# Retention of blocks 3 to 5 in 64x64 tiles: chunks worked by halves, in two groups of products

## The chip, the cores and the metric

One Trainium2 chip, one of its cores. The metric is the device time of one execution in microseconds. A core has five engines that run side by side, each in its own order: TensorE (PE: matmuls, and their weight loads, PEld), VectorE (DVE), ScalarE (ACT), GpSimd (POOL) and SyncE (SP), which here issues nearly all DMAs. Matmuls read SBUF and write PSUM.

## What is computed

Three layers in a row on 4 x 768 tokens of 512 values. The first is retention, 8 heads of 64 values each, one state per batch and head:

```python
for t in range(S):
    state = gamma * state + einsum('bhd,bhe->bhde', k[:, :, t], v[:, :, t])
    y[:, :, t] = scale * einsum('bhd,bhde->bhe', q[:, :, t], state)
```

Its output x (3072 x 512) goes through `g(x @ w_in) @ w_out` twice, w_in 512 x 2048 and w_out 2048 x 512. In layer 0 of the two g is a quotient of polynomials, `P(h) / (Q(h) + 1e-6)`; in layer 1 it is `h * clip(h + 3, 0, 6) / 6`.

## The kernel before

**Steps.** Tokens are worked in six blocks of 512 (NBLK), the 2048 inner columns in 16 tiles of 128 (FT). A step is one (layer, block, tile): `emit_h` (L359) makes h, 128x512 in PSUM, with 12 matmuls of 512 columns, and two steps later (LAG) `emit_o` (L371) adds the product of g with w_out into four accumulators with 12 more. Twelve and not four, since every operand is split into a rounded high part and a rest (xh, xl; gh, gl; two halves of each weight) and three of the four products are made. The steps stand in one list: 96 of layer 0, then 96 of layer 1. In layer 0 DVE and ACT turn h into g: ACT L440 to L442, DVE L448, L449, L452, ACT L457, L458 (`s1_h`, `s1_pq`, `s1_r`, one step behind h), DVE L463 to L465, ACT L470 (gh), DVE L476 (gl) (`s1_g`, `s_hi`, `s_lo`, two steps behind). h has two PSUM buffers, gh and gl two each.

**Retention.** A block has four chunks of 128 tokens, a sequence six chunks, so among the 12 chunks of blocks 3 to 5 two are the first and two the last of a sequence. A chunk is loaded by five DMAs of 256 KB on SP (`att_load`, L183: q and k transposed, k, v and a table of decays). `att_q` (L213) and `att_v` (L218) scale q and v by the decays on DVE. `att_scores` (L230) makes k.q for the eight heads, tiles of 64 rows and 128 columns, into the two PSUM banks of tag "at"; `att_mask` (L241) takes the triangle of it to SBUF, 1024 columns on DVE. `att_out` (L259) makes mask x v (L272, tiles of 128 rows and 64 columns), the chunk's sum of k x v (L285, same tiles, not in the last chunk) and state x q (L300, tiles of 64x64, not in the first). `att_xh` (L325, ACT) and `att_xl` (L337, DVE) write the chunk's part of the block's xh and xl, and `att_state` (L344) adds the sum to the state in SBUF. These products are fp32, and each is two matmul instructions in the profile.

**Order.** The order is written out by hand. `chunk_at` (L589) files each part of a chunk under a step n and a place in the step's program; the loop from L706 emits, for step n: `emit_h(n)`; what is filed under `begin`; `s1_g`, `s_hi` of tile n-2; `middle`; `s1_pq` of n-1 with `s_lo` of n-2 in it; `s1_r`; `before`; `emit_o(n-2)`; `after`. A chunk of blocks 3 to 5 that is filed at step s has its loads at s-2, q and v at s-1 (`before`), scores behind `emit_o` of s, mask in `before` of s+1, outputs behind `emit_o` of s+1, xh in `begin` and xl and state in `before` of s+2. The next chunk comes four steps later. The chunks of block b are worked during the steps of the block ahead of it in the list: from step n0 = 32, 48 and 64 for blocks 3, 4 and 5. The x tiles have two slots, b % 2 for these blocks.

Of the kernel before, what the change touches and what calls it, by code (L numbers as in the profile page):

```python
# [7 lines left out]
F32 = mybir.dt.float32  # L8
# [3 lines left out]
AF = mybir.ActivationFunctionType  # L12
# [19 lines left out]
def tile_retention_moe_moe2(  # L32
# [179 lines left out]

    def att_q(blk, c):  # L213
        qT, kT, kr, vr, tq, ka = loaded.pop((blk, c))
        nc.vector.tensor_tensor(out=qT, in0=qT, in1=tq, op=ALU.mult)
        attn[blk, c] = (by_pair(qT), by_pair(kT), heads(kr), heads(vr), ka)

    def att_v(blk, c):  # L218
        vr = attn[blk, c][3]
        powers = tab_v[(blk * CPB + c) % CPS]  # L220
        if (1, 0) < (blk, c) < (VIA + 1, 0):

            for h in range(H):
# [35 lines left out]
    def att_out(blk, c):  # L259
        qT, kr, vr, am = attn.pop((blk, c))  # L260
        ci = (blk * CPB + c) % CPS
        first, last = ci == 0, ci == CPS - 1
        both, py = two_banks(blk, (2 * c + 1) % 3, f"py{blk}_{c}")

        def to(e, j, i):
            return py[e][i * 64 : (i + 1) * 64, j * CH : (j + 1) * CH]

        for j in range(2):
            for e in range(2):
                for i in range(2):  # L270
                    p = 2 * j + i
                    nc.tensor.matmul(  # L272
                        to(e, j, i),
                        lhsT=vr[:, 2 * p + e, :],
                        rhs=am[:, e * NP + p, :],
                        start=j == 0,
                        stop=first and j == 1,
                        skip_group_check=True,
                    )
        new = py[0][:, 256:512]  # L280

        def to_state():
            for p in range(NP):
                for e in range(2):
                    nc.tensor.matmul(  # L285
                        new[e * 64 : (e + 1) * 64, p * D : (p + 1) * D],
                        lhsT=kr[:, 2 * p + e, :],
                        rhs=vr[:, 2 * p + e, :],
                        start=False,
                        stop=True,  # L290
                        skip_group_check=True,
                    )

        def from_state():
# [13 lines left out]


        parts = ([] if last else [to_state]) + ([] if first else [from_state])  # L310
        for part in reversed(parts) if (blk, c) == (0, CPB - 1) else parts:
            part()
        attn[blk, c] = (both, new, first, last)

    XSLOT = {0: 1, 1: 0, 6: 0, 7: 1, 8: 1, 9: 0, 10: 1, 11: 0} | {b: b % 2 for b in range(2, 6)}

# [94 lines left out]
    def emit_evac(layer, blk, f):  # L411
        earlier = partial.pop((layer, blk), None)
        for j, ps in enumerate(acc.pop((layer, blk))):
            scale = G_SCALE if layer == 0 else 1.0 / 6.0
            if earlier:
                o = earlier[j]
                nc.vector.scalar_tensor_tensor(out=o, in0=ps, scalar=scale, in1=o, op0=ALU.mult, op1=ALU.add)
            else:
                o = out_tile(layer, blk, j, f"o{layer}_{blk}_{f}_{j}")
                if layer == 0 or j % 2 == 0:  # L420
                    nc.scalar.activation(o, ps, AF.Copy, scale=scale)
                else:
                    nc.vector.tensor_scalar(out=o, in0=ps, scalar1=scale, scalar2=None, op0=ALU.mult)
            t0 = blk * NB + j * 128
            if layer == 0:
                to = x2_dram[blk][j]
            else:
                to = out[t0 : t0 + 128, :] if f == FT - 1 else part_dram[j]
            nc.sync.dma_start(out=to, in_=o)

    def s1_h(key):
# [4 lines left out]
        p = t2.tile([128, NB], F32, tag="p", name=f"p{nm}")  # L439
        nc.scalar.activation(p, h, AF.Identity, scale=ab[:, 3:4], bias=ab[:, 2:3])  # L440
        nc.scalar.activation(s, h, AF.Square)
        nc.scalar.activation(u, h, AF.Abs, scale=ab[:, 4:5])  # L442
        tm[key] = [s, u, p]

    def s1_pq(key, between=None):
        s, u, p = tm[key]
        h = hps.pop(key)
        nc.vector.tensor_tensor(out=p, in0=p, in1=h, op=ALU.mult)  # L448
        nc.vector.scalar_tensor_tensor(out=u, in0=s, scalar=babs[:, 1:2], in1=u, op0=ALU.mult, op1=ALU.add)  # L449
        if between:  # L450
            between()
        nc.vector.scalar_tensor_tensor(out=p, in0=p, scalar=ab[:, 1:2], in1=h, op0=ALU.add, op1=ALU.mult)  # L452

    def s1_r(key):
        s, u, p = tm[key]
        r = t1.tile([128, NB], F32, tag="r", name=f"r{key[1]}_{key[2]}")
        nc.scalar.activation(r, u, AF.Ln, scale=1.0 / LN_SCALE, bias=ln_bias)  # L457
        nc.scalar.activation(r, r, AF.Exp, scale=-1.0)  # L458
        tm[key] = [u, p, r]

    def s1_g(key):
        u, p, r = tm[key]
        nc.vector.scalar_tensor_tensor(out=u, in0=u, scalar=Q_CONST, in1=r, op0=ALU.add, op1=ALU.mult)  # L463
        nc.vector.scalar_tensor_tensor(out=p, in0=p, scalar=ab[:, 0:1], in1=r, op0=ALU.add, op1=ALU.mult)  # L464
        nc.vector.scalar_tensor_tensor(out=p, in0=u, scalar=-2.0 * LN_SCALE, in1=p, op0=ALU.add, op1=ALU.mult)  # L465
        tm[key] = p

    def s_hi(key):
# [4 lines left out]
    def s_lo(key):  # L473
        gh = gsp[key]
        gl = g_p.tile([128, NB], F32R, tag="gl", name="gl" + "_".join(map(str, key)))
        nc.vector.tensor_tensor(out=gl, in0=tm.pop(key), in1=gh.bitcast(F32), op=ALU.subtract)  # L476
        gsp[key] = (gh, gl)


# [101 lines left out]
            made["lo"] += 1  # L581


    begin, middle, before, after, begun = {}, {}, {}, {}, []

    def put(where, n, fn, *args):
        where.setdefault(n, []).append((fn, *args))
# [1 line left out]
    def chunk_at(blk, c, s, loads=None):  # L589
# [9 lines left out]
        put(middle if blk <= VIA else begin, s + 2, att_xh, blk, c)  # L599
        put(before, s + 2, att_evac, blk, c)  # L600

    for c in range(CPB):
        chunk_at(1, c, 2 * c - 1, max(2 * c - 3, -1))
        chunk_at(VIA, c, CUT1 + 4 * c, CUT1 - 2 + 4 * c)
        for b in range(VIA + 1, NBLK):
            n0 = at_of[0, b - 1, 0] if b > VIA + 1 else 2 * FT
            chunk_at(b, c, n0 + 4 * c, n0 + 4 * c - 2)
# [88 lines left out]
    w_hi(*jobs[1])  # L696
    nc.scalar.activation(babs, ab[:, 4:6], AF.Abs)
    att_state(0, 3)
    for parts in (begin, middle, before, after):
        for n in sorted(n for n in parts if n < 0):  # L700
            for fn, *args in parts.pop(n):
                if fn is not att_load:
                    begun.append((fn, *args))

    late = []
    for n in range(len(steps) + LAG):  # L706
# [7 lines left out]
        if n == 0:  # L714
# [1 line left out]
            w_second()  # L716
            w_first()
            emit_h(at_step(1))
        if k1:
            (s1_h, s2_h)[k1[0]](k1)  # L720
# [5 lines left out]
        if k2 and k2[0] == 0:  # L726
            s1_g(k2)
            s_hi(k2)
        elif k2:
            s_lo(k2)  # L730
        for fn, *args in middle.get(n, ()):
            fn(*args)
        for key in late:
# [2 lines left out]
        late.clear()  # L736
        while made["lo"] < made["bits"]:
            w_second()
        rest = (lambda: s_lo(k2)) if k2 and k2[0] == 0 else None
        if k1 and k1[0] == 1:  # L740
            if rest:
                rest()
            s2_g(k1)
            s_hi(k1)
        if todo > 0:
            w_first()
        if k1 and k1[0] == 0:
# [93 lines left out]
```

## Time and profile before

| | before |
|---|---|
| median of 3 runs | 1170.14 us (1169.34 to 1170.98) |
| span of the profiled execution | 1169.4 us |
| PE busy, matmul instructions | 1142.6 us, 6028 |
| DVE busy, instructions | 754.3 us, 1174 |
| ACT busy, instructions | 640.2 us, 1091 |
| POOL busy | 32.6 us |

The profile is of one execution, from its first to its last instruction; its time is 0.7 us under the median of the runs. Busy time of PE counts a matmul from its start until its last result, and one starts while the one before is still draining; so starts, not durations, tell its pace. The timeline merges equal instructions that follow each other: a start, the time until the last of them ends, and their count.

### The profile page before, as it was taken

How to read it: one execution, taken by the hardware profiler on the slowest of the kernel's cores; microseconds unless marked ns; L12 is line 12 of the kernel's file. 1: busy time of each engine (PE TensorE's matmuls, PEld its weight loads, DVE VectorE, ACT ScalarE, POOL GpSimd, SP SyncE). 2: the span in 40 equal slices, each digit the busy share in tenths (PEclk: the TensorE clock that was granted, in tenths of full speed). 3: DMA queues.
4: the chain of work that ended last, by engine and by line, in shares of the span. 5: the costliest groups of instructions: out<-in, count | busy, mean ns of one | idle time of the engine just before them, and what ended most of it. 6: DMA issues, size and time to landing. Idle time of an engine off the chain costs nothing.

```text
span 1169.4 us, 15740 instructions
## 1 busy us (share of the span) xinstructions
PE 1142.6 (98%) x6028; PEld 931.0 (80%) x6028; DVE 754.3 (64%) x1174; ACT 640.2 (55%) x1091; POOL 32.6 (3%) x43
## 2 busy tenths in 40 slices
PE   8698999999999999999999999999999999999998
PEld 5566788888888888888888788888888888888886
DVE  6898898998888878888899865432332332332322
ACT  3898888866666566666888644332222332332222
POOL 0121110000000000000000000000000000000000
PEclk9898999999999999999999999999999999999999
DMA  9898643312112113121332643120200200200000
GB/s 334 246 263 211 183 114 95 135 53 74 46 46 82 46 55 117 46 81 37 108 99 64 227 136 106 36 90 1 72 1 1 72 1 1 72 1 1 36 1 36
DMA packets 59547, 100.20 MB, mean 86 GB/s; under 512 B 5328, under 2 KB 23888, under 8 KB 59472
## 3 DMA queue, kind: packets, MB, share of 16 engines
q1 hardware_dynamic: 54144, 89.50, 23.2%
q0 software_dynamic: 5328, 9.70, 4.8%
q8 instruction: 47, 0.77, 0.3%
q14 instruction: 28, 0.23, 0.1%
HBM read 73.76 MB, written 15.73 MB: 77 GB/s over the span
## 4 chain that ended last, share of the span: by engine, by line
PE 80%; ACT 8%; DVE 7%; DMA 2%; issue 2%; SPq 0%; ACTq 0%; DVEq 0%
PE h L368 38%; PE accA L392 19%; PE accB L392 19%; DMA T<-in_qk_t_dram 2%; PE sc L236 1%; PE py L272 1%; DVE u L463 1%; ACT r L457 1%; DVE p L464 1%; DVE p L448 1%; ACT r L458 1%; DVE u L449 1%; PE py L300 1%; ACT p L440 1%; ACT u L442 1%
## 5 line engine op out<-in xcount | busy, mean ns | idle before, releaser
L368 PE MATMUL h<-xh,wi 128*128 128x512 f32 x1536 | 416.4, 393 | 0.9 <-ACT xh L335 0.9
L368 PEld LDWEIGHTS h<-xh,wi 128*128 128x128 f32 x1536 | 285.8, 188 | 63.9 <-issue 2.7
L368 PE MATMUL h<-xl,wi 128*128 128x512 f32 x768 | 205.7, 390 | 0.0
L488 DVE SCALAR_TENSOR_TENSOR g<-r,h 128x512 f32<-128x512 f32 x96 | 66.1, 688 | 169.4 <-ACT r L482 168.7
L368 PEld LDWEIGHTS h<-xl,wi 128*128 128x128 f32 x768 | 144.3, 188 | 30.7
L482 ACT ACTIVATE r<-h,cst 128x512 f32<-128x512 f32 x96 | 66.0, 687 | 183.6 <-PE h L368 183.1
L470 ACT ACTIVATE gh<-g 128x512 fp32r<-128x512 f32 x96 | 60.7, 632 | 153.1 <-PE accB L392 113.9
L476 DVE TENSOR_TENSOR gl<-g,gh 128x512 fp32r<-128x512 f32 x96 | 66.5, 693 | 120.3 <-ACT gh L470 120.3
L392 PE MATMUL accA<-gh,wo 128*128 128x512 f32 x384 | 120.5, 395 | 8.3 <-ACT gh L470 8.3
L392 PE MATMUL accB<-gh,wo 128*128 128x512 f32 x384 | 119.4, 392 | 0.0
L392 PE MATMUL accB<-wo,gh 128*128 128x512 f32 x384 | 118.3, 390 | 0.0
L392 PE MATMUL accA<-wo,gh 128*128 128x512 f32 x384 | 118.2, 389 | 0.0
L440 ACT ACTIVATE p<-h,ab 128x512 f32<-128x512 f32 x96 | 74.3, 774 | 38.5 <-PE h L368 35.3
L392 PEld LDWEIGHTS accA<-gh,wo 128*128 128x128 f32 x384 | 71.7, 189 | 26.7 <-ACT gh L470 12.5
L457 ACT ACTIVATE r<-u,cst 128x512 f32<-128x512 f32 x96 | 69.2, 721 | 38.2 <-DVE u L449 38.2
L476 DVE TENSOR_TENSOR gl<-p,gh 128x512 fp32r<-128x512 f32 x96 | 65.8, 685 | 33.3 <-ACT gh L470 33.1
L392 PEld LDWEIGHTS accB<-gh,wo 128*128 128x128 f32 x384 | 72.7, 189 | 15.4
L392 PEld LDWEIGHTS accB<-wo,gh 128*128 128x128 f32 x384 | 72.1, 188 | 15.0
L392 PEld LDWEIGHTS accA<-wo,gh 128*128 128x128 f32 x384 | 72.1, 188 | 14.9
L470 ACT ACTIVATE gh<-p 128x512 fp32r<-128x512 f32 x96 | 60.7, 632 | 35.1 <-DVE p L465 35.0
L448 DVE TENSOR_TENSOR p<-p,h 128x512 f32<-128x512 f32 x96 | 65.5, 682 | 16.3 <-ACT u L442 16.1
L392 PE MATMUL accA<-wo,gl 128*128 128x512 f32 x192 | 74.8, 389 | 0.0
(76 smaller groups left out, 1441.5 us busy)
## 6 DMA issues: line engine op xcount, KB each, us to landing
rwi<-in_moe_w_in_dram SPq DMA_DIRECT2D x32, 512.0 KB, 4.5
rwo<-in_moe_w_out_dram SPq DMA_DIRECT2D x32, 512.0 KB, 3.9
T<-in_qk_t_dram SPq DMA_DIRECT2D x48, 256.0 KB, 4.0
kv<-in_kv_dram SPq DMA_DIRECT2D x32, 256.0 KB, 4.8
x<-o SPq DMA_DIRECT2D x24, 256.0 KB, 2.4
xr<-x SPq DMA_DIRECT2D x24, 256.0 KB, 4.2
out_dram<-o SPq DMA_DIRECT2D x20, 256.0 KB, 2.0
wi<-rwi POOLq DMA_DIRECT2D x19, 256.0 KB, 3.8
```

What stands on the lines that cost most here:

```text
L236: nc.tensor.matmul(banks[e][:, p * CH : (p + 1) * CH], lhsT=kT[rows, p, :], rhs=qT[rows, p, :], start=True, stop=True)
L272: nc.tensor.matmul(to(e, j, i), lhsT=vr[:, 2 * p + e, :], rhs=am[:, e * NP + p, :], start=j == 0, stop=first and j == 1, skip_group_check= ...
L300: nc.tensor.matmul(to(e, j, i), lhsT=state[rows, p * D : (p + 1) * D], rhs=qT[rows, p, :], start=False, stop=j == 1, skip_group_check=True,)
L368: nc.tensor.matmul(ps, lhsT=w[:, cs], rhs=x[:, c, :], start=n == 0, stop=n == 3 * KD - 1)
L392: nc.tensor.matmul(acc[layer, blk][j], lhsT=l, rhs=r, start=f == f0 and i == 0, stop=f == f1 and i == 2)
L440: nc.scalar.activation(p, h, AF.Identity, scale=ab[:, 3:4], bias=ab[:, 2:3])
L448: nc.vector.tensor_tensor(out=p, in0=p, in1=h, op=ALU.mult)
L457: nc.scalar.activation(r, u, AF.Ln, scale=1.0 / LN_SCALE, bias=ln_bias)
L470: nc.scalar.activation(gh, tm[key], AF.Copy)
L476: nc.vector.tensor_tensor(out=gl, in0=tm.pop(key), in1=gh.bitcast(F32), op=ALU.subtract)
L482: nc.scalar.activation(r, hps[key], AF.Relu, bias=three)
L488: nc.vector.scalar_tensor_tensor(out=g, in0=r, scalar=6.0, in1=h, op0=ALU.min, op1=ALU.mult)
```

## The change

For blocks 3 to 5 a chunk is split into two halves of 64 tokens. Let S be the state ahead of the chunk, s = 0 and 1 its halves. The first group on PE makes the sums of k x v of each half and only the scores within a half; DVE makes two states, after half 0 and after half 1, in the tile of the decays (tq), and the mask is then 512 columns. The second group makes all products of the output: mask x v in each half, S x q for half 0, the state after half 0 x q for half 1. Each 64x64 tile of PE takes its operands from one half of the rows (heads e, or half s) and writes to one half of the partitions, and two row halves are kept to different PSUM banks; where head e and half s don't agree ("crossed"), the state product goes to free columns (`rest`), is copied by ACT to SBUF (`ret_rest`) and added to the output by DVE (`ret_join`). ACT copies the last state back (`ret_keep`).

A chunk is filed two steps earlier (n0 - 2 + 4c), its q and v in the step of its first group; the loads go to `middle` of s-2, copies, joins, keep and xh to `middle` of s+2, xl to `before` of s+2. The constant BEHIND is 10**6, more than there are steps: `soon(key)` is false and `old(key)` true for every key of layer 0, so that the branches on them in `s1_h`, `s1_pq`, `s1_g`, `s_lo`, `emit_evac` and the loop (left out here) emit what was emitted before, in the same order.

```diff
+    HALF = CH // 2
+    def tri_halves():
+        nc.scalar.activation(tri[HALF:CH, 0:HALF], tri[HALF:CH, HALF:CH], AF.Copy)
+    def ret_banks(blk, c, name):
+        both = ps_at.tile([128, 1024], F32, tag="at", name=f"{name}{blk}_{c}")
+        halves = both.rearrange("p (b t) -> p b t", b=2)
+        return halves[:, :, 0:256], halves[:, :, 256:512]
...
+    def ret_load(blk, c):
+        att_load(blk, c, (3, 2, 0, 4, 1))
+    def ret_first(blk, c):
...
+        for p in range(NP):
+            for s in range(1 if last else 2):
+                ts = slice(s * HALF, (s + 1) * HALF)
+                for e in range(2):
+                    nc.tensor.matmul(
+                        new[e * 64 : (e + 1) * 64, s, p * D : (p + 1) * D],
+                        lhsT=kr[ts, 2 * p + e, :],
+                        rhs=vr[ts, 2 * p + e, :],
...
+        for p in range(NP):
+            for e in range(2):
+                rows = slice(e * 64, (e + 1) * 64)
+                for s in range(2):
+                    ts = slice(s * HALF, (s + 1) * HALF)
+                    nc.tensor.matmul(
+                        sc[ts, e, p * HALF : (p + 1) * HALF],
+                        lhsT=kT[rows, p, ts],
+                        rhs=qT[rows, p, ts],
...
+    def ret_states(blk, c):
+        tq = states[blk, c]
...
+            nc.vector.tensor_tensor(out=tq[:, 0:256], in0=state, in1=new[:, 0, :], op=ALU.add)
+        if not last:
+            nc.vector.tensor_tensor(out=tq[:, 256:512], in0=tq[:, 0:256], in1=new[:, 1, :], op=ALU.add)
+    def ret_mask(blk, c):
+        qT, kT, kr, vr, ka = attn.pop((blk, c))
+        am = ka[:, 0:512].rearrange("p (e a t) -> p e a t", e=2, t=HALF)
+        nc.vector.tensor_tensor(
+            out=am,
+            in0=score.pop((blk, c))[0].rearrange("p e (a t) -> p e a t", t=HALF),
...
+    def ret_to(py, e, j, i, s):
+        return py[i * 64 : (i + 1) * 64, s, (2 * e + j) * HALF : (2 * e + j + 1) * HALF]
+    def ret_before(blk, c, py, qT, pairs, rest=None):
+        for j in range(2):
+            for i in range(2):
+                p = 2 * j + i
+                for e, s in pairs:
+                    rows = slice(e * 64, (e + 1) * 64)
+                    nc.tensor.matmul(
+                        ret_to(py, e, j, i, s) if rest is None else ret_to(rest, 0, j, i, e),
+                        lhsT=(state, states[blk, c])[s][rows, p * D : (p + 1) * D],
+                        rhs=qT[rows, p, s * HALF : (s + 1) * HALF],
...
+    def ret_out(blk, c):
...
+        for j in range(2):
+            for e in range(2):
+                for s in range(2):
+                    ts = slice(s * HALF, (s + 1) * HALF)
+                    for i in range(2):
+                        nc.tensor.matmul(
+                            ret_to(py, e, j, i, s),
+                            lhsT=vr[ts, 4 * j + 2 * i + e, :],
+                            rhs=am[ts, e, 2 * j + i, :],
...
+        ret_before(blk, c, py, qT, ([] if first else [(0, 0)]) + [(1, 1)])
+        ret_before(blk, c, py, qT, [(0, 1)] + ([] if first else [(1, 0)]), rest)
...
+    def ret_rest(blk, c):
...
+            to = am[:, 0:256].rearrange("p (e t) -> p e t", e=2)
+            nc.scalar.activation(to, rest[:, :, 0:128], AF.Copy)
+        attn[blk, c] = (py, to)
+    def ret_join(blk, c):
+        py, rest = attn[blk, c]
+        for e, s in [(0, 1)] + ([] if place(blk, c)[0] else [(1, 0)]):
+            cols = slice(128 * e, 128 * (e + 1))
+            nc.vector.tensor_tensor(out=py[:, s, cols], in0=py[:, s, cols], in1=rest[:, e, :], op=ALU.add)
...
+    def ret_keep(blk, c):
+        if not place(blk, c)[1]:
+            nc.scalar.activation(state, states[blk, c][:, 256:512], AF.Copy)
...
+    def chunk_by_halves(blk, c, s):
+        def at(n, where, fn):
+            put(early if n >= BEHIND else where, n, fn, blk, c)
+        put(middle, s - 2, ret_load, blk, c)
+        at(s, before, att_v)
+        at(s, before, att_q)
+        put(after, s, ret_first, blk, c)
+        at(s + 1, middle, ret_states)
+        at(s + 1, before, ret_mask)
+        put(after, s + 1, ret_out, blk, c)
+        at(s + 2, middle, ret_rest)
+        at(s + 2, middle, ret_join)
+        at(s + 2, middle, ret_keep)
+        at(s + 2, middle, ret_xh)
+        at(s + 2, before, ret_xl)
+    put(before, 2 * FT - 6, tri_halves)
...
+                chunk_by_halves(b, c, n0 - 2 + 4 * c)
```

## Rows read from the trace of the kernel before

**Rows 1.** The page: busy time of each engine, share of the span, instructions.

```profile
PE 1142.6 (98%) x6028; PEld 931.0 (80%) x6028; DVE 754.3 (64%) x1174; ACT 640.2 (55%) x1091; POOL 32.6 (3%) x43
```

**Rows 2.** Busy time by stretch; behind POOL: granted clock, DMA share, GB/s.

```profile
250.00:540.00 290.00, 290.00 (x1801) 235.79 (x1800) 246.76 (x380) 182.55 (x294) 0.00 (x0) 1.00 0.20 67
540.00:800.00 260.00, 259.45 (x1141) 213.40 (x1140) 183.61 (x295) 157.82 (x264) 6.89 (x8) 1.00 0.33 100
800.00:1169.00 369.00, 365.09 (x1611) 302.10 (x1609) 106.87 (x157) 98.79 (x153) 0.00 (x0) 1.00 0.07 23
```

**Rows 3.** Timeline of PE, a middle chunk: start us, us, engine, line, operation.

```profile
472.65 1.07 PE L368 MATMUL h<-xh,wi 128*128 128x512 f32 x4
...
478.18 1.16 PE L236 MATMUL sc<-T 64*128 64x128 f32 x16
479.28 1.19 PE L368 MATMUL h<-xh,wi 128*128 128x512 f32 x4
...
484.40 0.61 PE L392 MATMUL accB<-gl,wo 128*128 128x512 f32 x2
484.94 1.09 PE L272 MATMUL py<-T,kv 128*64 128x128 f32 x16
485.87 0.63 PE L285 MATMUL py<-kv 128*64 128x64 f32 x16
486.43 0.67 PE L300 MATMUL py<-T,state 64*64 64x128 f32 x16
487.03 1.19 PE L368 MATMUL h<-xh,wi 128*128 128x512 f32 x4
...
492.62 1.07 PE L368 MATMUL h<-xh,wi 128*128 128x512 f32 x4
...
498.06 1.07 PE L368 MATMUL h<-xh,wi 128*128 128x512 f32 x4
```

**Rows 4.** Timeline of PE: around the outputs of a first and a last chunk.

```profile
403.67 1.19 PE L368 MATMUL h<-xh,wi 128*128 128x512 f32 x4
...
410.83 1.19 PE L368 MATMUL h<-xh,wi 128*128 128x512 f32 x4
...
530.09 1.20 PE L368 MATMUL h<-xh,wi 128*128 128x512 f32 x4
...
537.38 1.19 PE L368 MATMUL h<-xh,wi 128*128 128x512 f32 x4
```

**Rows 5.** PE: groups by form, 250 to 540 us; timeline of 486.43 to 486.46.

```profile
L300 PE MATMUL py<-T,state 64*64 64x128 f32 x160 | 6.7, 282 | 0.0
L285 PE MATMUL py<-kv 128*64 128x64 f32 x160 | 6.3, 222 | 0.0
...
486.43 0.34 PE L300 MATMUL py<-T,state 64*64 64x128 f32 x4
```

**Rows 6.** Line 236 in 525.58 to 525.63 us; DVE's timeline ahead of it.

```profile
L236 PEldq EVENT_SEMAPHORE  x1: 51/51/51, 525.6 to 525.6; - x1
...
524.88 0.68 DVE L476 TENSOR_TENSOR gl<-p,gh 128x512 fp32r<-128x512 f32 x1
```

**Rows 7.** Timeline of DVE and PE around the scores of a chunk.

```profile
527.87 0.69 DVE L465 SCALAR_TENSOR_TENSOR p<-u,p 128x512 f32<-128x512 f32 x1
528.00 0.62 PE L392 MATMUL accA<-gl,wo 128*128 128x512 f32 x2
...
528.48 0.68 DVE L448 TENSOR_TENSOR p<-p,h 128x512 f32<-128x512 f32 x1
...
529.00 1.16 PE L236 MATMUL sc<-T 64*128 64x128 f32 x16
...
529.74 0.69 DVE L476 TENSOR_TENSOR gl<-p,gh 128x512 fp32r<-128x512 f32 x1
...
534.76 0.62 PE L392 MATMUL accA<-gl,wo 128*128 128x512 f32 x2
```

**Rows 8.** Groups by form, 250 to 540 us: count, busy, mean ns, idle before.

```profile
L247 DVE TENSOR_TENSOR T<-sc,tab 128x1024 f32<-128x1024 f32 x12 | 14.6, 1215 | 0.0
L342 DVE TENSOR_TENSOR xl<-py,xh 128x512 fp32r<-128x512 f32 x12 | 8.2, 683 | 0.0
L335 ACT ACTIVATE xh<-py 128x512 fp32r<-128x512 f32 x12 | 7.2, 598 | 29.8 <-PE py L300 25.1 <-PE py L285 4.7
L349 DVE TENSOR_TENSOR state<-state,py 128x256 f32<-128x256 f32 x8 | 3.3, 411 | 0.0
```

**Rows 9.** The page's DMA issues: KB each, us from issue to landing.

```profile
T<-in_qk_t_dram SPq DMA_DIRECT2D x48, 256.0 KB, 4.0
```

More of the change, by code (lines that the diff above doesn't have):

```diff
@@ L20 @@
 CUT1, CUT2 = 8, 8
+BEHIND = 10**6
 LAG = 2
@@ L214, in att_q @@
         qT, kT, kr, vr, tq, ka = loaded.pop((blk, c))
+        states[blk, c] = tq
         nc.vector.tensor_tensor(out=qT, in0=qT, in1=tq, op=ALU.mult)
@@ L313, in att_out, with place @@
         attn[blk, c] = (both, new, first, last)
+    HALF = CH // 2
[5 more added lines that the diff above has]
+        return halves[:, :, 0:256], halves[:, :, 256:512]
+    def place(blk, c):
+        ci = (blk * CPB + c) % CPS
+        return ci == 0, ci == CPS - 1
@@ new lines, in ret_load @@
+    def ret_load(blk, c):
+        att_load(blk, c, (3, 2, 0, 4, 1))
+    def ret_first(blk, c):
+        qT, kT, kr, vr, ka = attn[blk, c]
+        sc, new = ret_banks(blk, c, "sc")
+        last = place(blk, c)[1]
+        for p in range(NP):
[6 more added lines that the diff above has]
+                        rhs=vr[ts, 2 * p + e, :],
+                        start=p == 0,
+                        stop=True,
+                        skip_group_check=True,
+                    )
+        for p in range(NP):
[7 more added lines that the diff above has]
+                        rhs=qT[rows, p, ts],
+                        start=p == 0 and last and e == 1,
+                        stop=True,
+                        skip_group_check=True,
+                    )
+        score[blk, c] = (sc, new)
@@ new lines, in ret_states @@
+    def ret_states(blk, c):
+        tq = states[blk, c]
+        new = score[blk, c][1]
+        first, last = place(blk, c)
+        if first:
+            nc.vector.tensor_copy(out=tq[:, 0:256], in_=new[:, 0, :])
+        else:
+            nc.vector.tensor_tensor(out=tq[:, 0:256], in0=state, in1=new[:, 0, :], op=ALU.add)
[7 more added lines that the diff above has]
+            in0=score.pop((blk, c))[0].rearrange("p e (a t) -> p e a t", t=HALF),
+            in1=tri[:, 0:HALF].unsqueeze(1).unsqueeze(1).to_broadcast([128, 2, NP, HALF]),
+            op=ALU.mult,
+        )
+        attn[blk, c] = (qT, vr, am)
@@ new lines, in ret_to @@
+    def ret_to(py, e, j, i, s):
[10 more added lines that the diff above has]
+                        rhs=qT[rows, p, s * HALF : (s + 1) * HALF],
+                        start=False,
+                        stop=True,
+                        skip_group_check=True,
+                    )
@@ new lines, in ret_out @@
+    def ret_out(blk, c):
+        qT, vr, am = attn.pop((blk, c))
+        first = place(blk, c)[0]
+        py, rest = ret_banks(blk, c, "py")
+        for j in range(2):
[7 more added lines that the diff above has]
+                            rhs=am[ts, e, 2 * j + i, :],
+                            start=(j, e) == (0, 0),
+                            stop=first and s == 0,
+                            skip_group_check=True,
+                        )
+        ret_before(blk, c, py, qT, ([] if first else [(0, 0)]) + [(1, 1)])
+        ret_before(blk, c, py, qT, [(0, 1)] + ([] if first else [(1, 0)]), rest)
+        attn[blk, c] = (py, rest, am.rearrange("p e a t -> p (e a t)"))
@@ new lines, in ret_rest @@
+    def ret_rest(blk, c):
+        py, rest, am = attn[blk, c]
+        if place(blk, c)[0]:
+            to = am[:, 0:128]
+            nc.scalar.activation(to, rest[:, 0, 0:128], AF.Copy)
+            to = to.unsqueeze(1)
+        else:
+            to = am[:, 0:256].rearrange("p (e t) -> p e t", e=2)
[6 more added lines that the diff above has]
+            nc.vector.tensor_tensor(out=py[:, s, cols], in0=py[:, s, cols], in1=rest[:, e, :], op=ALU.add)
@@ new lines, in ret_split, with ret_y, ret_xh @@
+    def ret_split(t):
+        return t.rearrange("p k (s t) -> p s k t", s=2)
+    def ret_y(blk, c):
+        return attn[blk, c][0].rearrange("p s (k t) -> p s k t", t=HALF)
+    def ret_xh(blk, c):
+        xs = slice(c * CH, (c + 1) * CH)
+        if blk == VIA:
+            xf = o_p.tile([128, 512], F32, tag="osb", name=f"xf{blk}_{c}")
+            nc.scalar.activation(ret_split(by_pair(xf)), ret_y(blk, c), AF.Copy)
+            nc.sync.dma_start(out=x_dram[:, :, xs].rearrange("a p t -> p a t"), in_=by_pair(xf))
+        else:
+            if c == 0:
+                x_tiles(blk)
+            nc.scalar.activation(ret_split(xin[blk][0][:, :, xs]), ret_y(blk, c), AF.Copy)
@@ L315, in tile_retention_moe_moe2, with ret_xl @@
+    def ret_keep(blk, c):
+        if not place(blk, c)[1]:
+            nc.scalar.activation(state, states[blk, c][:, 256:512], AF.Copy)
+    def ret_xl(blk, c):
+        if blk != VIA:
+            xh, xl = (ret_split(x[:, :, c * CH : (c + 1) * CH]) for x in xin[blk])
+            nc.vector.tensor_tensor(out=xl, in0=ret_y(blk, c), in1=xh.bitcast(F32), op=ALU.subtract)
+        attn.pop((blk, c))
+    states = {}
     XSLOT = {0: 1, 1: 0, 6: 0, 7: 1, 8: 1, 9: 0, 10: 1, 11: 0} | {b: b % 2 for b in range(2, 6)}
@@ L419, in emit_evac @@
                 o = out_tile(layer, blk, j, f"o{layer}_{blk}_{f}_{j}")
-                if layer == 0 or j % 2 == 0:
+                if j % 2 == 0 or layer == 0 and at_of[layer, blk, f] + 2 < BEHIND:
                     nc.scalar.activation(o, ps, AF.Copy, scale=scale)
@@ L429, in emit_evac, with soon, old, beside @@
             nc.sync.dma_start(out=to, in_=o)
+    def soon(key):
+        return key and key[0] == 0 and at_of[key] >= BEHIND
+    def old(key):
+        return key and key[0] == 0 and at_of[key] < BEHIND
+    def beside(key):
+        return nc.gpsimd if soon(key) else nc.vector
     def s1_h(key):
@@ L439, in s1_h @@
         p = t2.tile([128, NB], F32, tag="p", name=f"p{nm}")
+        if soon(key):
+            nc.scalar.activation(s, h, AF.Abs)
         nc.scalar.activation(p, h, AF.Identity, scale=ab[:, 3:4], bias=ab[:, 2:3])
-        nc.scalar.activation(s, h, AF.Square)
-        nc.scalar.activation(u, h, AF.Abs, scale=ab[:, 4:5])
+        if soon(key):
+            nc.scalar.activation(u, s, AF.Identity, scale=babs[:, 1:2], bias=babs[:, 0:1])
+        else:
+            nc.scalar.activation(s, h, AF.Square)
+            nc.scalar.activation(u, h, AF.Abs, scale=ab[:, 4:5])
         tm[key] = [s, u, p]
@@ L446, in s1_pq @@
         s, u, p = tm[key]
-        h = hps.pop(key)
+        h = hps[key] if soon(key) else hps.pop(key)
+        if soon(key):
+            nc.gpsimd.tensor_tensor(out=u, in0=s, in1=u, op=ALU.mult)
         nc.vector.tensor_tensor(out=p, in0=p, in1=h, op=ALU.mult)
-        nc.vector.scalar_tensor_tensor(out=u, in0=s, scalar=babs[:, 1:2], in1=u, op0=ALU.mult, op1=ALU.add)
+        if not soon(key):
+            nc.vector.scalar_tensor_tensor(out=u, in0=s, scalar=babs[:, 1:2], in1=u, op0=ALU.mult, op1=ALU.add)
         if between:
             between()
-        nc.vector.scalar_tensor_tensor(out=p, in0=p, scalar=ab[:, 1:2], in1=h, op0=ALU.add, op1=ALU.mult)
+        to = h if soon(key) else p
+        nc.vector.scalar_tensor_tensor(out=to, in0=p, scalar=ab[:, 1:2], in1=h, op0=ALU.add, op1=ALU.mult)
     def s1_r(key):
@@ L462, in s1_g @@
         u, p, r = tm[key]
+        q = hps.pop(key) if soon(key) else p
         nc.vector.scalar_tensor_tensor(out=u, in0=u, scalar=Q_CONST, in1=r, op0=ALU.add, op1=ALU.mult)
-        nc.vector.scalar_tensor_tensor(out=p, in0=p, scalar=ab[:, 0:1], in1=r, op0=ALU.add, op1=ALU.mult)
-        nc.vector.scalar_tensor_tensor(out=p, in0=u, scalar=-2.0 * LN_SCALE, in1=p, op0=ALU.add, op1=ALU.mult)
+        nc.vector.scalar_tensor_tensor(out=q, in0=q, scalar=ab[:, 0:1], in1=r, op0=ALU.add, op1=ALU.mult)
+        nc.vector.scalar_tensor_tensor(out=p, in0=u, scalar=-2.0 * LN_SCALE, in1=q, op0=ALU.add, op1=ALU.mult)
         tm[key] = p
@@ L475, in s_lo @@
         gl = g_p.tile([128, NB], F32R, tag="gl", name="gl" + "_".join(map(str, key)))
-        nc.vector.tensor_tensor(out=gl, in0=tm.pop(key), in1=gh.bitcast(F32), op=ALU.subtract)
+        beside(key).tensor_tensor(out=gl, in0=tm.pop(key), in1=gh.bitcast(F32), op=ALU.subtract)
         gsp[key] = (gh, gl)
@@ L581, in w_second @@
             made["lo"] += 1
-    begin, middle, before, after, begun = {}, {}, {}, {}, []
+    early, begin, middle, before, after, begun = {}, {}, {}, {}, {}, []
     def put(where, n, fn, *args):
@@ L600, in chunk_at @@
         put(before, s + 2, att_evac, blk, c)
+    def chunk_by_halves(blk, c, s):
[14 more added lines that the diff above has]
+    put(before, 2 * FT - 6, tri_halves)
     for c in range(CPB):
         chunk_at(1, c, 2 * c - 1, max(2 * c - 3, -1))
[L604 to L607, printed above, removed]
+    for b in range(VIA, NBLK):
+        n0 = at_of[0, b - 1, 0] if b > VIA + 1 else 2 * FT
+        for c in range(CPB):
+            if b == VIA:
+                chunk_at(b, c, CUT1 + 4 * c, CUT1 - 2 + 4 * c)
+            else:
+                chunk_by_halves(b, c, n0 - 2 + 4 * c)
     for key in (VIA, *range(NBLK, 2 * NBLK)):
@@ L698, in tile_retention_moe_moe2 @@
     att_state(0, 3)
-    for parts in (begin, middle, before, after):
+    for parts in (early, begin, middle, before, after):
         for n in sorted(n for n in parts if n < 0):
@@ L718, in tile_retention_moe_moe2 @@
             emit_h(at_step(1))
-        if k1:
-            (s1_h, s2_h)[k1[0]](k1)
+        for fn, *args in early.get(n, ()):
+            fn(*args)
+        if old(k2) and soon(k1):
+            s1_g(k2)
+            s_hi(k2)
+            s_lo(k2)
+        if soon(k1):
+            for key in late:
+                emit_evac(*key)
+            late.clear()
+            s1_r(k1)
+            s1_g(k1)
+        elif old(k1):
+            s1_h(k1)
+        elif k1:
+            s2_h(k1)
         for key in late:
@@ L725, in tile_retention_moe_moe2 @@
             fn(*args)
-        if k2 and k2[0] == 0:
+        if old(k2) and not soon(k1):
             s1_g(k2)
             s_hi(k2)
-        elif k2:
+        elif k2 and k2[0] == 1:
             s_lo(k2)
+        if soon(cur):
+            s1_h(cur)
+        if soon(k1):
+            s_hi(k1)
         for fn, *args in middle.get(n, ()):
@@ L738, in tile_retention_moe_moe2 @@
             w_second()
-        rest = (lambda: s_lo(k2)) if k2 and k2[0] == 0 else None
+        if old(k2) and not old(k1):
+            s_lo(k2)
         if k1 and k1[0] == 1:
-            if rest:
-                rest()
             s2_g(k1)
@@ L746, in tile_retention_moe_moe2 @@
             w_first()
-        if k1 and k1[0] == 0:
-            s1_pq(k1, rest)
+        if old(k1):
+            s1_pq(k1, (lambda: s_lo(k2)) if k2 else None)
             s1_r(k1)
+        if soon(cur):
+            s1_pq(cur)
+        if soon(k1):
+            s_lo(k1)
         if todo > 1:
```

2 lines of the change are left out of this document (1 added, 1 removed).

## The prediction

> **What bounds the kernel now.** I read the page's shares first: TensorE (PE) is busy 98% of the span and no other engine over 64% [rows 1]. The table by stretches then says where the change lies: the twelve chunks of blocks 3 to 5 are worked between 250 and 540 us, PE is busy there for all 290 us at a granted clock of 1.00, VectorE (DVE) for 247 and ScalarE (ACT) for 183; from 540 on PE is still full to within 5 us of 629, and DVE thins out [rows 2]. So a microsecond taken off PE before 540 comes off the end, as long as DVE and ACT, which make gh and gl for every step, keep up. The timeline of PE gives the unit [rows 3]: a plain step, h then o, is 24 matmuls of 512 columns and takes 5.44 us (492.62 to 498.06). A chunk adds three things: the step that ends in scores takes 479.28 - 472.65 = 6.63 (1.19 more), the step that ends in outputs takes 7.75 (2.31 more), and the h behind it loses 0.15 (487.03 to 492.62 is 5.59). That is 3.65 us of PE per chunk with nothing beside it. The first chunk of a sequence adds no term from the state and its output step takes 7.16; the last makes no new state and its takes 7.29 [rows 4]. With the same 1.19 and 0.15 they cost 3.06 and 3.19. Eight middle, two first and two last chunks: 29.2 + 6.1 + 6.4 = **41.7 us**.
>
> **PE after.** An fp32 product is two matmul instructions (8 products, x16 in the rows). What sets their pace? With two tiles side by side and 128 columns (L272) the 16 take 1.09, less the first's extra 0.05 and the 0.27 of the last one, 0.77 over 7 pairs: 0.11 a pair. With two tiles and 64 columns (L285): 0.63 - 0.22 over 7 pairs, 0.058. With four tiles and 128 columns (L300): 0.67 - 0.05 - 0.27 over 3 sets of four, 0.11 a set [rows 3, 5]. So columns set the period, and the number of tiles does not. The new products are all 64x64 tiles with 64 columns, and their loops go through four different tiles in turn, so I take 0.058 for a set of four. Instructions: a middle chunk has 32 for the sums, 32 for the scores, 32 + 32 + 32 for the outputs, 160; the last of a sequence 144 (16 for sums), the first 128 (16 + 16 from its own state, on two tiles only). Together 8 x 160 + 2 x 144 + 2 x 128 = 1824, against 704 now. 1792 go in 448 sets, 32 in 16 pairs: 464 x 0.058 = 26.9 us. Each of the 24 groups also pays for its change of tile shape: 0.09 late at entry (the next matmul was due at 484.85, L272 starts at 484.94), 0.05 for its first load, 0.11 after its last set (L300's four sets end 0.11 before h starts at 487.03) and 0.15 in h: 0.40, and 9.6 in all. Scores and outputs each stay in one shape, where now the output changes once more on the way (L285 to L300). Sum **36.5 us, 5.2 less**. A period of 0.055, half the 128-column one, would give another 1.4; the upper end is the fastest mean the rows show, 0.027 per matmul or 0.107 a set, which is the first rival below.
>
> **DVE and ACT, beside PE.** Removed: the mask of 1024 columns, 1.22, and the one state sum of 0.41 behind each output [rows 8]. Added on DVE: a mask of 512 columns (0.68, as xl's), two state sums of 0.41 that hang on each other, and two joins of 128 columns; from 0.41 at 256 and 0.68 at 512 columns a line gives 0.27 each, 0.41 is the upper end. In starts from one to the next that is 0.3 us more DVE a chunk, on 21 to 22 in 25 us [rows 2]. Added on ACT: rest (256 columns from PSUM) and keep (256 columns), each between nothing and the 0.60 that xh takes at 512 [rows 8]; I take 0.4, two thirds of xh for half its columns. ACT is at 63%, so their time costs nothing by itself. The waits matter more. The state sums stand between L465 and L448 of the step after the scores, and DVE is there at 528.5, while PE starts the group at 529.00 [rows 7]; the sums need 0.14 + 8 x 0.058 + 0.2 of it, so DVE stands some 1.3 us with L448, L449, gl and L452 queued behind. In the next step the join waits for ACT's rest, and that for the last output product: when I lay one chunk's instructions out by these durations DVE has 2 us of waiting there, and 0.8 left at the sums, as it is later by then. That is 3.3 us a chunk with the waits for Exp, and the DVE has 25 - 21.7 = 3.3 idle. Cover: the gl made at 529.74 to 530.42 is first used at 534.76, 4 us later [rows 7]; that made at 524.88 to 525.56 by 528.00, 2.4 us [rows 6, 7]. In my layout about 1.8 us of this is left at the tightest step. What comes late next if that goes is gl, and PE would stand before its last four matmuls of o. On the other side xh, which now holds ACT before gh (29.8 us of idle in the stretch) [rows 8], goes behind gh. I take a loss of 0.3 in all, for the step where block 0's four sums are written and q, v now fall too.
>
> **Moves that cost nothing.** Everything runs two steps, 11 us, earlier; the x slot it writes was last read one step before. q and v are scaled in the step of their scores, not the one before, and end about 2 us before PE asks. The five loads per chunk are issued from SP two steps ahead as now (11 us against 4.0 to land) [rows 9]; the table's and k's part wait for keep and join, and SP has no weights to load in this stretch. The one copy of a triangle corner is under 0.4 on ACT. The new order for steps at or after BEHIND is not reached, and the rest of the loop comes out as it was.
>
> **Sum.** 5.2 - 0.3 = 4.9 us less. The profiled execution has a span of 1169.4, 0.7 under the median of 1170.14; on the median: **1165.2**.
>
> **Rivals.** (1) *PE cannot be fed.* 160 instructions and as many loads a chunk, in groups of 64 and 96, need 0.0145 us per matmul; no row shows a mean below 0.027 (L285, L300). If that is a limit of issue, a set takes 0.107: 464 x 0.107 + 9.6 = 59.2, 17.5 more, **1187.6**, slower. It decides from a period of (41.7 - 9.6) / 464 = 0.069; at 0.08 the time is 1175. Against it: four matmuls of 0.32 fill only 0.34, so they start within 0.02 [rows 5]; and the queue reaches the semaphore instruction ahead of L236 less than 0.07 after the gl that ends at 525.56 [rows 6], with four loads and four matmuls on gl in between: under 0.009 per instruction with the wake-up, where 0.0073 is needed. That is close, and every row for it is eight instructions long. Chance 0.17.
> The Trainium skill, "TensorE: Matmul & The Clock Gate" (section "Wait — 56ns, not 53.3ns?"), says that start-to-start never drops below about 25 ns however few the columns, which speaks against this change: an estimate by that figure is 1824 x 0.025 + 9.6, 55 us, and 1184. The four starts within 0.02 disagree with it for neighbouring tiles; for a long run no row decides.
> (2) *DVE takes the gain.* If the waits for the sums and the join are 2 us longer than laid out (dearer joins and rest, later semaphores), gl is late at each chunk and PE stands 0.2 to 0.6: **1168 to 1172**, no change. For it: 85% busy and two new waits; against: the cover above. Chance 0.14.
> (3) *The four tiles do not overlap*, and go as pairs: 912 x 0.058 + 9.6 = 62.5, **1191**. L300 has the same tiles and overlaps; the new groups differ in that both row halves write columns of the same tile, in two banks. Chance 0.03.
> (4) *Cheaper than summed*: period 0.055 and 0.33 a change: **under 1163.5**. Chance 0.05.
>
> **How the numbers follow.** The forecast keeps 0.61, with its own range 1163.5 to 1167.5. A measurement here tells 0.2%, 2.3 us, from no change. Faster: 0.61 + 0.05; same: 0.14; slower: 0.17 + 0.03. Below 1163.5 lies 0.05; to leave no more than 0.15 above, the range takes in (2) and the mild third of (1), to 1174.
>
> **What would show it.** PE instructions 6028 + 1120 = 7148. On PE's timeline the step with sums and scores should take 6.6 to 6.7 us and the one with outputs 7.1; the sets should start 0.058 apart. Wrong if those groups last 1.8 and 2.6 (rival 1), or if PE shows waits for gl L476 or gh L470 in the steps behind a chunk (rival 2). On DVE waits for PE at the state sums (near 0.8) and for ACT at the join (near 2) should appear, without PE idling for them.

## The result and the profile after

The changed kernel takes **1160.45 us** (median of 4 runs, 1159.42 to 1162.08) against 1169.74 for the kernel before in the same runs: a ratio of 0.9913, 95% interval 0.9901 to 0.9925. That is 9.3 us less by the medians, and 8.8 to 11.6 by the interval. The prediction had the sign and the stage, and 1165.2: 4.9 us less, about half.

The page, busy time per engine, to set against [rows 1]:

```profile
PE 1131.7 (98%) x6796; PEld 922.4 (80%) x6796; DVE 758.1 (65%) x1208; ACT 646.9 (56%) x1114; POOL 32.6 (3%) x43
```

PE has 768 matmul instructions more, and 10.9 us less to do. The forecast had 1120 more. So the first line of the page already shows the step that failed.

The busy times of one stretch, from the h of step 28 to the h of step 80, first in the kernel before, then in the changed one (columns: length; PE, PEld, DVE, ACT, POOL busy; granted clock, DMA share, GB/s):

```profile
223.94:548.39 324.45, 324.45 (x1953) 264.34 (x1952) 279.32 (x430) 207.64 (x335) 0.00 (x0) 1.00 0.19 64
```

```profile
222.85:537.06 314.21, 314.21 (x2721) 256.58 (x2720) 282.96 (x465) 213.74 (x357) 0.00 (x0) 1.00 0.21 66
```

The same 52 steps, and all 12 chunks, take 10.2 us less; PE is busy throughout in both at the full clock, and DVE and ACT have 3.6 and 6.1 us more to do. From the h of step 80 to the last h the two kernels take the same 605.7 us. The spans (1169.4 and 1158.2) differ by 11.2 us; the rest of that lies in steps 8 to 27, 131.7 us before and 130.6 after, where nothing but the one copy of the triangle's corner differs. In the runs below that leave these steps as they are, they take 129.9 to 132.2 us, so this 1.1 us is not put down to the change.

The timeline over a middle chunk, PE and the joins on DVE, to set against [rows 3]:

```profile
452.99 1.07 PE L526 MATMUL h<-xh,wi 128*128 128x512 f32 x4
...
458.53 0.69 PE L343 MATMUL sc<-kv 64*64 64x64 f32 x32
459.04 0.65 PE L356 MATMUL sc<-T 64*64 64x64 f32 x32
459.62 1.19 PE L526 MATMUL h<-xh,wi 128*128 128x512 f32 x4
...
465.29 0.69 PE L415 MATMUL py<-T,kv 64*64 64x64 f32 x32
465.80 0.22 PE L397 MATMUL py<-T,state 64*64 64x64 f32 x2
...
466.38 1.19 PE L526 MATMUL h<-xh,wi 128*128 128x512 f32 x4
466.93 0.63 DVE L442 TENSOR_TENSOR py<-py,T 128x128 f32<-128x128 f32 x2 [1.19 <-ACT T L435]
...
471.95 1.07 PE L526 MATMUL h<-xh,wi 128*128 128x512 f32 x4
```

The step with sums and scores takes 459.62 - 452.99 = 6.63, as before (1.19 over a plain step); the step with outputs 6.76 (1.32 over, where it was 2.31); the h behind it loses 0.13. A chunk costs PE 2.64 us in place of 3.65. L415 starts at 465.29 and L397 at 465.80, so 32 instructions of four tiles take 0.51 with their first load. No step of the stretch is longer than its like: the 0.3 us that the prediction set aside as lost is not lost.

Groups by form between 236 and 520 us (count, busy, mean ns, idle before):

```profile
L415 PE MATMUL py<-T,kv 64*64 64x64 f32 x384 | 8.3, 224 | 0.0
L397 PE MATMUL py<-T,tq 64*64 64x64 f32 x192 | 7.1, 219 | 0.0
L442 DVE TENSOR_TENSOR py<-py,T 128x128 f32<-128x128 f32 x22 | 6.6, 299 | 14.7 <-ACT T L435 12.6 <-ACT T L431 1.8
L397 PE MATMUL py<-T,state 64*64 64x64 f32 x160 | 6.5, 218 | 0.0
L373 DVE TENSOR_TENSOR tq<-state,sc 128x256 f32<-128x256 f32 x10 | 4.2, 420 | 5.9 <-PE sc L356 5.9
L463 ACT ACTIVATE state<-tq 128x256 f32<-128x256 f32 x10 | 4.1, 408 | 0.0
L435 ACT ACTIVATE T<-py 128x256 f32<-128x256 f32 x10 | 3.8, 383 | 1.9 <-PE py L397 1.1
```

The products of the states (L397) are 192 + 160 = 352 instructions; the prediction counted 704. The two new DVE waits are there, at the joins (L442, 14.7 us in all) and at the state sums (L373, 5.9; mostly 0.9 a chunk, nothing in some), and PE waits for neither gl nor gh in the stretch: its list of waits between 240 and 535 us is empty. L373 waits for the end of the scores (L356), not of the sums it reads, which the layout had supposed.

### The profile page after: what moved, and what is told of

The parts are those of the page before. It is cut to its first block, busy times and chain, and to the rows that moved or that the text cites. A ratio compares the mean times of both kernels' runs of the same rounds, so it can differ in the third digit from the quotient of the medians.

```text
span 1158.2 us, 17351 instructions
## 1 busy us (share of the span) xinstructions
PE 1131.7 (98%) x6796; PEld 922.4 (80%) x6796; DVE 758.1 (65%) x1208; ACT 646.9 (56%) x1114; POOL 32.6 (3%) x43
## 4 chain that ended last, share of the span: by engine, by line
PE 76%; ACT 10%; DVE 8%; DMA 3%; issue 3%; ACTq 0%; SPq 0%; DVEq 0%; POOLq 0%
PE h L526 36%; PE accA L550 18%; PE accB L550 18%; DVE u L640 1%; ACT r L633 1%; DVE p L641 1%; ACT r L634 1%; DVE p L622 1%; DVE u L624 1%; ACT p L609 1%; DMA rwo<-in_moe_w_out_dram 1%; DVE p L642 1%; PE warm L847 1%; DMA T<-in_qk_t_dram 1%; ACT u L614 1%
## 5 line engine op out<-in xcount | busy, mean ns | idle before, releaser
L550 PE MATMUL accB<-wo,gl 128*128 128x512 f32 x192 | 74.7, 389 | 0.0
L640 DVE SCALAR_TENSOR_TENSOR u<-u,r 128x512 f32<-128x512 f32 x96 | 65.9, 686 | 12.8 <-ACT r L634 12.8
```

Of the source, the lines that this page charges most:

```text
L550: nc.tensor.matmul(acc[layer, blk][j], lhsT=l, rhs=r, start=f == f0 and i == 0, stop=f == f1 and i == 2)
```

## The experiments

Each kernel is the changed one with one edit. "The stretch" is the one from step 28 to step 80, 314.2 us in the changed kernel and 324.5 before. Ratios are to the kernel before in the same runs.

**The number of products.** `ret_again` repeats `ret_before` into columns of `rest` that nothing reads:

```diff
         ret_before(blk, c, py, qT, [(0, 1)] + ([] if first else [(1, 0)]), rest)
+        ret_again(blk, c, qT, ([] if first else [(0, 0)]) + [(1, 1)], rest, 64)
+        ret_again(blk, c, qT, [(0, 1)] + ([] if first else [(1, 0)]), rest, 64)
```

> Sixteen products of the second group (state x q, own and crossed) are made a second time into free columns, so that a middle chunk has the 160 matmul instructions that the prediction counted (the program makes 128). Theory, the count alone was wrong: 96 more sets or pairs at 0.058 us, 5.6 us more than the changed kernel's 1160.5: 1166, about the predicted 1165.2. Rival, the gain has another source or long groups are fed more slowly: at 0.107 a set 10 us more, 1171; with no cost for them 1160.5.

It took 1165.97 us, ratio 0.9958 (0.9942 to 0.9974), and 319.3 in the stretch, 5.1 more. The timeline of PE shows the repeats behind the group's own products:

```profile
419.45 0.69 PE L430 MATMUL py<-T,kv 64*64 64x64 f32 x32
419.97 0.23 PE L397 MATMUL py<-T,state 64*64 64x64 f32 x2
...
420.43 0.22 PE L412 MATMUL py<-T,state 64*64 64x64 f32 x2
...
421.01 1.19 PE L543 MATMUL h<-xh,wi 128*128 128x512 f32 x4
```

From L397 to L412 it is 0.46 us for 8 sets, 0.058 a set, and a group of 96 is fed as fast as one of 64. The page counts 7148 PE instructions, as many as the prediction, and the kernel takes the time that it predicted (1165.2). The cause of the miss is the count.

**Half the columns.** The same repeats with `qT[rows, p, s * HALF : s * HALF + 32]` into 32 columns:

> The same repeated products, but of 32 columns instead of 64 (half of each repeated product is left out; the output doesn't use them). If columns alone set the period: 0.029 a set, 2.8 us over the changed kernel, 1163.3. If the weight load of 64 columns or the issue sets it: 0.058, 5.6 us, 1166, as with 64 columns.

1164.80 us, ratio 0.9951 (0.9933 to 0.9969), 319.0 in the stretch. The timeline of PE from 419.42 on:

```profile
419.42 0.20 PE L412 MATMUL py<-T,state 64*64 64x32 f32 x2
419.43 0.20 PE L412 MATMUL py<-T,tq 64*64 64x32 f32 x2
419.45 0.23 PE L412 MATMUL py<-T,state 64*64 64x32 f32 x2
419.46 0.23 PE L412 MATMUL py<-T,tq 64*64 64x32 f32 x2
419.51 0.23 PE L412 MATMUL py<-T,state 64*64 64x32 f32 x2
```

Only the second set follows after 0.03; from then on a set starts each 0.06, as with 64 columns, and 12 times 0.03 is about all that this kernel is shorter than the one above in the stretch. So 0.058 isn't the time of 64 columns alone; something that 32 columns leave as it is, the weight load or the issue, holds it there. The two were not told apart. The Trainium skill, "TensorEngine Tiling (Array Packing)" (section "Performance Considerations"), says that a matmul has the same latency with one column as with about 60; the pace in this trace agrees, 0.06 a set at 32 and at 64.

**The order of the tiles.** The scores of one tile one after the other:

```diff
-        for p in range(NP):
-            for e in range(2):
-                rows = slice(e * 64, (e + 1) * 64)
-                for s in range(2):
+        for e in range(2):
+            rows = slice(e * 64, (e + 1) * 64)
+            for s in range(2):
+                for p in range(NP):
```

> The scores' loops are turned, so that the four products of one 64x64 tile follow each other instead of four tiles in turn; the same products. Theory, the four tiles overlap only in turn: 32 instructions at 0.058 in place of 8 sets, 1.4 us a chunk, 16.7 us in all: 1177. Rival, the order doesn't matter (the engine picks free tiles): 1160.5.

1170.31 us, ratio 0.9994 (0.9984 to 1.0003): the whole gain is gone by the order of one loop nest. Its timeline differs from that of the changed kernel by 0.84 us a chunk here, and by 0.04 in the step with outputs:

```profile
415.64 1.49 PE L356 MATMUL sc<-T 64*64 64x64 f32 x32
417.06 0.50 PE L526 MATMUL h<-xh,wi 128*128 128x512 f32 x1
```

The group takes 1.42 where it took 0.58 (459.04 to 459.62). The loss is 0.84 us and not 1.4: 0.041 an instruction. The single starts in the trace say why. The first tile's products start 0.058 apart, at 415.64, 415.70 and so on, and the next tile's first starts at 415.88, when three of the eight are still to come. So a tile's last products overlap the next tile's first, and the theory had the direction. In the changed kernel the products of one tile also start 0.058 apart: the period is one tile's own, and four tiles in turn run it side by side.

**The place in the order.** `chunk_by_halves(b, c, n0 + 4 * c)`, two steps later:

> Every chunk filed two steps later, as in the kernel before (n0 + 4c). Theory, the two steps cost and give nothing: 1160.5, within 1. Rival, a part of the gain is from the earlier place: 2 us or more lost, 1162.5 and up.

1160.89 us, ratio 0.9914 (0.9898 to 0.9930), 315.0 in the stretch: at most 0.8 us of the gain is from the earlier place. All of it lies in steps 34 and 35 (6.06 and 5.78 us, 5.59 and 5.44 for their like), where block 0's four sums on DVE now stand right behind the first chunk's join. In the changed kernel the same sums meet q and v of the next chunk, for which the prediction took its 0.3, and no step is longer.

**DVE's spare time.** Operations on columns of the mask that nothing reads any more, ahead of the joins, here 6:

```diff
+        free = spare[blk, c]
+        for _ in range(6):
+            nc.vector.tensor_tensor(out=free, in0=free, in1=free, op=ALU.min)
         for e, s in [(0, 1)] + ([] if place(blk, c)[0] else [(1, 0)]):
```

> Two idle DVE operations of 256 columns (0.41 us, 0.33 from start to start) ahead of each join: 0.7 us more DVE per chunk. Theory, DVE has 1.8 us to spare at its tightest step: 1160.5. Rival, DVE already decides: 0.7 x 12 = 8 us more, 1168.5.

> Six of these operations, 2.0 us more DVE per chunk. Theory: the spare 1.8 us is just used up, 0 to 0.4 us a chunk, 1160.5 to 1165. Rival, DVE decides throughout: 24 us more, 1184.

> Ten of these operations, 3.4 us more DVE per chunk. Theory: 1.3 to 1.6 us a chunk over what is spare, 16 to 19 us more, 1176 to 1180. If nothing is lost even here (1160.5), the cover was much larger than laid out.

1161.20, 1171.65 and 1197.15 us; ratios 0.9918 (0.9903 to 0.9933), 1.0004 (0.9995 to 1.0013) and 1.0226 (1.0209 to 1.0243). In the stretch it is 0.1, 10.7 and 37.9 us more. The timeline of DVE, with the h on PE, in the kernel with six:

```profile
425.37 2.72 DVE L443 TENSOR_TENSOR T<-T 128x256 f32<-128x256 f32 x6 [0.17 <-PE py L415]
425.70 1.19 PE L531 MATMUL h<-xh,wi 128*128 128x512 f32 x4
428.01 0.63 DVE L446 TENSOR_TENSOR py<-py,T 128x128 f32<-128x128 f32 x2
...
431.58 1.08 PE L531 MATMUL h<-xh,wi 128*128 128x512 f32 x4
...
437.33 1.07 PE L531 MATMUL h<-xh,wi 128*128 128x512 f32 x4
```

and in the one with ten:

```profile
524.34 1.19 PE L531 MATMUL h<-xh,wi 128*128 128x512 f32 x4
528.49 0.62 DVE L446 TENSOR_TENSOR py<-py,T 128x128 f32<-128x128 f32 x2
...
532.07 1.09 PE L531 MATMUL h<-xh,wi 128*128 128x512 f32 x4
...
537.80 1.07 PE L531 MATMUL h<-xh,wi 128*128 128x512 f32 x4
```

Each reads what the one before wrote and takes 0.44, not the 0.33 expected: 0.9, 2.6 and 4.4 us in all (2.64 from 425.37 to 428.01). Two of them fit into the wait for rest (14.7 us over 12 chunks, 1.2 each). In a plain middle chunk the join starts 0.55 behind the h of its step in the changed kernel (466.38 to 466.93). With six it is 2.31, so 1.76 later, and this step and the next are 0.6 longer together (425.70 to 437.33, against 5.57 + 5.44); with ten it is 4.15, 3.6 later, and they are 2.45 longer. Both leave 1.15 us that was to spare beyond the wait, and all that goes beyond it is lost. The tightest steps are those in which a block's last products are added (49 and 65): they need gl earlier. With six such a step takes 6.4 to 6.5 us in place of 5.44, which with the 0.3 lost in the step ahead of it leaves 0.3 to 0.4 to spare, and not the 1.8 of the prediction. These steps and the ones around block 0's sums (33 to 37) make up the rest of the 10.7 us. With ten, PE waits for gl (PE's waits, 250 to 570 us: us, times, longest):

```profile
PE accA L555 <- DVE gl L658: 23.9, 15, 2.5
```

Behind four of these waits the granted clock is 0.50 for 3.4 us, as in 448.80 to 452.20; it is 1.00 throughout the stretch in the changed kernel.

**Block 2 as well.** `chunk_by_halves(b, c, CUT1 + 4 * c)` for b == VIA, the triangle's copy at step 7:

> Block 2's four chunks by halves too, in their old place (steps 8 to 23). Theory, 1.0 us of PE per chunk: 4 us less, 1156.5, if PE sets the end there; in that stretch two steps of the kernel before take 5.6 to 10.5 us each, so PE waits there for weights, and 0 to 4 less is expected: 1156.5 to 1160.5. Rival, the joins and sums are too much for DVE beside the weights: 2 us or more slower.

1164.26 us, ratio 0.9940 (0.9924 to 0.9957): slower than the changed kernel by 3.8. With q and v a step ahead:

> Block 2's chunks by halves as in the run before, but with q and v scaled a step ahead of their products, as the kernel before has it. Theory, the loss came from ACT's eight scalings of v ahead of the first group: 2 to 4 us come back, 1160 to 1162, and at best PE's saving of 4 us shows, 1157. Rival, the sums and joins themselves hold DVE and ACT up beside the weights: 1164 as before.

1165.74 us, ratio 0.9955 (0.9938 to 0.9971). Steps 8 to 27 take 135.6 and 137.1 us in these two. PE's waits in steps 8 to 24 (90 to 210 us) are, in the changed kernel, in the first of these two and in the second:

```profile
PE accA L550 <- ACT gh L647: 5.1, 2, 3.8
```

```profile
PE accA L550 <- DVE gl L653: 3.6, 3, 1.7
PE accA L550 <- ACT gh L647: 3.0, 1, 3.0
```

```profile
PE accA L550 <- ACT gh L647: 8.5, 4, 5.4
PE accA L550 <- DVE gl L653: 3.6, 3, 1.7
```

PE waits there for gh already (not for weights, as the expectation had it), and now for gl too, right behind the sums and joins. The saving is there where nothing holds PE: step 13, with outputs, takes 6.76 in both and 7.75 in the changed kernel. The theory on v's scalings named a real wait, but moving them only moved it. In step 16 of the first kernel, ACT's eight scalings hold the sums, 1.77 us in place of 0.51:

```profile
157.25 2.00 ACT L226 ACTIVATE kv<-kv,tab 128x64 f32<-128x64 f32 x8
157.70 1.94 PE L343 MATMUL sc<-kv 64*64 64x64 f32 x31
```

In the second they stand ahead of gh, and PE waits for that instead:

```profile
153.67 2.01 ACT L226 ACTIVATE kv<-kv,tab 128x64 f32<-128x64 f32 x8
157.97 0.73 PE L550 MATMUL accA<-gh,wo 128*128 128x512 f32 x2 [1.03 <-ACT gh L647]
160.92 0.69 PE L343 MATMUL sc<-kv 64*64 64x64 f32 x32
```

In these steps, where PE doesn't set the end, taking matmul time off it in exchange for work on DVE and ACT cost time. No version tried is faster than the changed kernel.

**The price of a change of shape.** The second group parted in two, its products of the states a step later, with rest, joins and xh behind them:

```diff
         put(after, s + 1, ret_out, blk, c)
+        put(after, s + 2, ret_out_state, blk, c)
-        at(s + 2, middle, ret_rest)
+        at(s + 3, middle, ret_rest)
...
```

> The second group is parted: products of the mask a step earlier than those of the states, so that each chunk changes the tile shape three times in place of two; rest, joins and xh come a step later. Nothing else is added. Theory, a change of shape costs 0.40 us: 12 x 0.40 = 4.8 us more, 1165.3. Rival, the drain is hidden behind the matmuls on either side and only durations of small products count: 1160.5.

1165.13 us, ratio 0.9952 (0.9937 to 0.9967), and 319.2 in the stretch: 5.0 us more, 0.42 a group. Of it 0.46 us is one step (34, 7.08 us against 6.62) and no change of shape; a middle chunk takes 0.38 more. The Trainium skill, "TensorEngine Tiling (Array Packing)" (section "Tiling Modes"), says that a change of tiling mode drains the engine; the 0.38 us for the way in and out fits that, and whether it is a drain no row shows. In the timeline 32 instructions alone take 0.62 up to the next h, of which 0.46 are sets; the rest of the 0.38 is at the entry (0.09) and in the h behind (0.14).

```profile
444.80 0.69 PE L415 MATMUL py<-T,kv 64*64 64x64 f32 x32
445.42 1.19 PE L531 MATMUL h<-xh,wi 128*128 128x512 f32 x4
```

## Why the prediction was wrong

**The step that failed** is the count of instructions in "PE after": "a middle chunk has 32 for the sums, 32 for the scores, 32 + 32 + 32 for the outputs, 160". `ret_before` walks four pairs of heads and two pairs of (e, s): 8 products, 16 instructions a call, and not 16 products. State x q is 8 heads in 2 halves, 16 products in all, own and crossed together. A middle chunk has 32 + 32 + 32 + 16 + 16 = 128 instructions, a first and a last one 112: 8 x 128 + 4 x 112 = 1472, and 1472 - 704 = 768 is what the page shows. By the text's own method: first and last chunks have 16 instructions each that use two tiles (the prediction had the last chunk's sums among the sets of four), so 4 x 8 = 32 pairs and (1472 - 64) / 4 = 352 sets, 384 x 0.058 = 22.3, with 9.6 for the changes of shape 31.9. Against 41.7 that is 9.8 less, with the 0.3 taken off 9.5: 1160.6. Measured: 1160.45. That the two agree so closely is partly luck, for in the stretch 10.2 us went, with no loss of 0.3. The miscounted 704 - 352 = 352 instructions are what the repeats put back, and they bring 1165.97.

Point by point:
- *What bounds the kernel*: right. All of the gain is in the stretch named, and what PE saves there (10.2) comes off the end.
- *The period of 0.058*: right (0.058). The reason given, that columns set it, holds from 64 to 128 and no longer at 32; that the number of tiles doesn't set it is right.
- *0.40 for a change of shape*: right (0.38 in a middle chunk).
- *Four tiles only in turn*: the loops' order is what gives it; one nest turned costs 9.9 us.
- *DVE and ACT*: joins 0.30 for 0.27, rest 0.38 and keep 0.41 for 0.4; 0.3 us more DVE a chunk is right (3.6 in all). The waits were laid out at 2 us (join) and 0.8 (sums); they are 1.2 and 0.6 in the mean. The spare time at the tightest step was put at 1.8 and is 0.3 to 0.4 beyond the wait. So the waits were sized too long and the cover too thick, and that the first offset the second is luck. With six small operations a chunk the time is that of rival (2).
- *A loss of 0.3* where block 0's sums are written: none.
- *The move by two steps costs nothing*: right, and it gives up to 0.8 us. SP does load weights near the end of the stretch (from 494 us on in the changed kernel), other than the text says, and no step there is longer.
- *Rival (1), PE cannot be fed*: false. 64 instructions from 458.53 to 459.62 take 0.017 each with the way in and out, and 96 in a group go at the same pace. The rule of the Trainium skill ("TensorE: Matmul & The Clock Gate", section "Wait — 56ns, not 53.3ns?") of 25 ns from start to start does not hold for four tiles in turn: 0.058 / 4 is 14.5 ns.
- *Rival (3)*: false, the four overlap. *Rival (4)*, under 1163.5, came out in number, not in its reason: period and change of shape were as summed.

The forecast "the step with outputs 7.1" would have named the fault by itself: it is 6.76 (7.23 with the repeats), and the groups' counts say why.

## What to carry to other kernels

Before durations are multiplied, check the count against what the mathematics needs: 8 heads in 2 halves are 16 products, whatever the loops look like. Where PE sets the end, small products pay by sets of tiles in turn and by changes of shape, and both can be read off a kernel that has other small products. The same rewrite lost in the steps where PE waits for other engines. Work that DVE does while it waits anyway costs nothing: 0.9 us a chunk ahead of the joins was free here, and 2.6 took the whole gain.

## What the runs showed of the hardware

- But for the second set of a run, matmuls of 32 columns in 64x64 tiles follow each other no faster than those of 64: sets 0.06 apart in both (0.11 at 128 columns [rows 3, 5]).
- Products of one tile start 0.058 us apart, alone or beside three other tiles. With the tile's products in a row an instruction costs 0.041 us, against 0.0145 in turn.
- In the last chunk of a sequence 16 instructions for sums take as long as 32, as they use one row half (PE's timeline; in a middle chunk L343 and L356 take 1.09 together):

```profile
361.10 0.62 PE L343 MATMUL sc<-kv 64*64 64x64 f32 x14
361.51 0.27 PE L356 MATMUL sc<-T 64*64 64x64 f32 x2
361.56 0.23 PE L343 MATMUL sc<-kv 64*64 64x64 f32 x2
361.61 0.63 PE L356 MATMUL sc<-T 64*64 64x64 f32 x30
362.18 1.19 PE L526 MATMUL h<-xh,wi 128*128 128x512 f32 x4
```

  From 361.10 to 362.18 is 1.08, with 16 instructions fewer.
